# A softmax region reordered: the short last piece of q and k first, the square root by log and exp, no diagonal matrices

## The chip, the cores and the metric

The kernel runs on one core of a Trainium2 chip. The metric is the device time of one execution in microseconds; the kernel before was run three times. Engines: PE multiplies matrices (its weight loads are listed as PEld), DVE is VectorE, ACT ScalarE, SP the engine that issues most DMAs.

## What is computed

```python
qn = q / (norm(q, axis=tokens) + 1e-6)        # q, k, v: 6080 x 256
kn = k / (norm(k, axis=tokens) + 1e-6)
s = kn.T @ qn / tau                           # 256 x 256
a = softmax(s)                                # rows, sum + 1e-9
x = v @ a                                     # 6080 x 256
x = square(relu(x @ w_in_1)) @ w_out_1        # 256 -> 2048 -> 256
h = x @ w_in_2
out = (h * clip(h + 3, 0, 6) / 6) @ w_out_2
```

## The kernel before

The weights arrive as 64-bit floats. Each half of a 512-column block of them is loaded by SP (L269) into one of two buffers (tag `w64`) and made single precision by a *conversion* of three background steps: Abs and a scaled copy on ACT (L135, L136), clamp and shift on DVE (L123, L127), add and sign on DVE (L139, L131). The sign step still reads the raw words, so a buffer is free for the next load when it has run. Halves of `w_out` have two steps more: the rounded part `hi` on ACT (L105) and the remainder `lo` on DVE (L295).

**Score region.** q and k come in pieces of 2, then 4, then 3 and 2 tiles of 128 rows, and a last short one of 64 rows. For each tile PE adds k^T q into two PSUM tiles (L510; one such 32-bit matmul is two records in the trace), ACT squares (L535, L538), DVE adds the squares up (L111). After a piece `STEPS` says how many background steps run. The matmuls of the last 4 tiles are held back (`HELD`).

**Softmax region.** Square sums by PE (L560), guard (L566), square root on ACT (L568), one Newton step and reciprocals on DVE, two diagonal matrices (L579), from which PE makes the row `factor` (L584); the held scores fill PE. Then per half `dh`: scale (L599), maximum (L601), Exp with its sum (L602), two transposes (L610), a copy to `e_sb` (L611). `attn_w(u)` multiplies the softmax matrix with block `w1[u]` of the first weights (L442, four products); `take` (L449) scales the result into the block `wblk`, and `hi[a]`, `lo[a]` split it into the slots of `w_ops[0, u]`. `parts` and the rest's steps prepare the data's slots in the same way from `blk`. Background steps stand between all this at five places (`FILL`).

**Steps.** After that the kernel runs (phase, chunk, u, p) steps. A step of the first kind has 24 products with `w_ops` (`mul`, L712), squares of Relu (L744 to L748), `hi` and `lo` of the result, and 24 products of the step before with `w_out` (L654), in the order that `out_mms` gives: the first ones use the second half of `w_out`'s block. In step 0 there is no step before; the four products of `attn_w(1)` are put in its place, spread by `AW_POPS`. Step 1 starts with `need(("o", 0))`, the conversions of `w_out`'s block 0.

**Order.** PE, SP and GpSimd run in the order of the program throughout. In the softmax region ACT and DVE do too, up to `ordered.close()`; behind it the planner places their work by readiness and then by order, and may put it into gaps ahead. `background(n)` takes the next n steps of two alternating tasks; `beside` inside a step calls it for a share of what is due; `need(name)` runs a task to its end. A task's load is issued when it becomes one of the first two.

## Time and profile before

| | us |
|---|---|
| median of three runs | 1073.31 (1073.2 to 1073.48) |
| span of the profiled execution, first to last instruction | 1071.5 |
| PE busy | 1064.3 (99%) |
| DVE busy | 889.3 (83%) |
| ACT busy | 640.7 (60%) |

The span is that of one profiled execution; a run's time has some 1.8 us around it. PE's busy time counts pipelined matmuls, so it doesn't show short waits; they are read from the distance of its records and from the waits of its weight loads.

### The profile page before, as it was taken

The page shows a single profiled execution, that of the slowest core. Times are in us where ns is not written, and L with a number is a line of the kernel's source. Part 1 is how long each engine was busy: PE and PEld are TensorE (multiplying, and loading weights), DVE is VectorE, ACT ScalarE, POOL GpSimd, SP SyncE. Part 2 cuts the span into 40 slices and gives each one's busy share as a digit, 9 for nine tenths or more (in the row PEclk, how much of TensorE's full clock was granted, in tenths as well). Part 3 has the DMA queues.
Part 4 walks back from the last instruction along what each step waited for, and adds up shares of the span by engine and source line. Part 5 has one row for each costly group of instructions (what it writes and reads, how often), then busy time and mean ns, then how long its engine had stood idle before and what let it go on. Part 6 is the DMA issues. An engine that isn't in the chain of part 4 may idle for free.

```text
span 1071.5 us, 12778 instructions
## 1 busy us (share of the span) xinstructions
PE 1064.3 (99%) x4602; PEld 866.0 (81%) x4602; DVE 889.3 (83%) x1510; ACT 640.7 (60%) x1111; POOL 9.4 (1%) x22
## 2 busy tenths in 40 slices
PE   9999999999999999999999999999999999999998
PEld 8777788888888888888888888888888888888886
DVE  5999958877887987887868988898898898898785
ACT  6699756666666567666555455455555555555443
POOL 0000000000000000000100000000000000000000
PEclk9999999999999999999999999999999999999999
DMA  9624302113132113115435002002002001001001
GB/s 356 247 93 143 98 20 69 60 62 115 50 115 81 50 59 132 45 59 197 138 137 186 1 0 78 1 1 78 1 1 79 1 1 61 18 0 39 1 1 39
DMA packets 33567, 78.03 MB, mean 73 GB/s; under 512 B 3296, under 2 KB 16864, under 8 KB 33504
## 3 DMA queue, kind: packets, MB, share of 16 engines
q1 hardware_dynamic: 27024, 57.49, 16.2%
q0 software_dynamic: 2304, 11.54, 3.2%
q10 hardware_dynamic: 4176, 8.19, 2.1%
q8 instruction: 36, 0.59, 0.2%
q14 instruction: 27, 0.22, 0.1%
HBM read 53.22 MB, written 23.99 MB: 72 GB/s over the span
## 4 chain that ended last, share of the span: by engine, by line
PE 95%; DMA 3%; DVE 1%; ACT 1%; issue 0%; SPq 0%; ACTq 0%; DVEq 0%
PE y L654 50%; PE s L712 44%; DMA q<-q_dram 2%; PE s L442 1%; DMA k<-k_dram 1%; ACT sq L538 0%; PE aw L442 0%; DVE acck L111 0%; DVE accq L111 0%; ACT cv L136 0%; DVE mx L601 0%; DVE sc L599 0%; DVE w L131 0%; DVE ct L139 0%; DVE b L108 0%
## 5 line engine op out<-in xcount | busy, mean ns | idle before, releaser
L654 PE MATMUL y<-g,oh 128*128 128x506 f32 (+1 forms) x1536 | 507.5, 392 | 0.0
L712 PE MATMUL s<-b,wh 128*128 128x506 f32 (+1 forms) x1360 | 424.8, 394 | 0.0
L108 DVE TENSOR_TENSOR g<-h,g 128x506 fp32r<-128x506 f32 (+1 forms) x384 | 262.4, 684 | 106.7 <-ACT g L105 98.7
L654 PEld LDWEIGHTS y<-g,oh 128*128 128x128 f32 x1536 | 289.5, 189 | 64.0 <-DVE g L108 0.4
L712 PEld LDWEIGHTS s<-b,wh 128*128 128x128 f32 x1360 | 255.9, 188 | 61.0 <-issue 1.9
L654 PE MATMUL y<-g,ol 128*128 128x506 f32 (+1 forms) x768 | 302.3, 394 | 0.0
L712 PE MATMUL s<-b,wl 128*128 128x506 f32 (+1 forms) x680 | 267.5, 393 | 0.0
L105 ACT ACTIVATE g<-h 128x506 fp32r<-128x506 f32 (+1 forms) x384 | 235.3, 622 | 38.1 <-DVE h L757 14.1
L105 ACT ACTIVATE u<-s 128x506 f32<-128x506 f32 (+1 forms) x176 | 104.6, 594 | 134.7 <-PE s L712 134.7
L654 PEld LDWEIGHTS y<-g,ol 128*128 128x128 f32 x768 | 144.7, 188 | 31.5
L712 PEld LDWEIGHTS s<-b,wl 128*128 128x128 f32 x680 | 128.4, 189 | 28.2 <-DVE wl L108 0.2
L111 DVE TENSOR_TENSOR h<-u,s 128x506 f32<-128x506 f32 (+1 forms) x176 | 119.5, 679 | 23.7 <-ACT u L105 22.3
L105 ACT ACTIVATE m<-s 128x506 f32<-128x506 f32 (+1 forms) x88 | 52.3, 595 | 114.4 <-PE s L712 113.9
L740 DVE SCALAR_TENSOR_TENSOR h<-r,h 128x506 f32<-128x506 f32 (+1 forms) x144 | 98.9, 687 | 4.9
L736 DVE SCALAR_TENSOR_TENSOR h<-h 128x506 f32<-128x506 f32 (+1 forms) x120 | 81.9, 683 | 1.4
L756 ACT ACTIVATE r<-s,three 128x506 f32<-128x506 f32 (+1 forms) x48 | 32.9, 685 | 60.3 <-PE s L712 59.9
L111 DVE TENSOR_TENSOR h<-m,s 128x506 f32<-128x506 f32 (+1 forms) x88 | 59.9, 680 | 8.0 <-PE s L712 3.2
L739 DVE TENSOR_SCALAR r<-h 128x506 f32<-128x506 f32 (+1 forms) x144 | 60.6, 421 | 1.7
L108 DVE TENSOR_TENSOR b<-blk,b 128x506 fp32r<-128x506 f32 (+1 forms) x81 | 55.0, 681 | 0.0
L105 ACT ACTIVATE b<-blk 128x506 fp32r<-128x506 f32 (+1 forms) x81 | 49.5, 615 | 0.4 <-DMA blk<-vT_dram 0.4
L753 ACT ACTIVATE r<-s 128x506 f32<-128x506 f32 (+1 forms) x40 | 23.8, 594 | 38.1 <-PE s L712 34.0
L510 PE MATMUL sc<-q,k 128*128 128x256 f32 x192 | 43.3, 384 | 0.7 <-DMA q<-q_dram 0.5
(85 smaller groups left out, 495.4 us busy)
## 6 DMA issues: line engine op xcount, KB each, us to landing
w<-w_in_dram SPq DMA_DIRECT2D x16, 512.0 KB, 4.7
w<-w_out_dram SPq DMA_DIRECT2D x16, 512.0 KB, 3.8
k<-k_dram SPq DMA_DIRECT2D x10, 512.0 KB, 7.4
blk<-vT_dram SPq DMA_DIRECT2D x8, 506.0 KB, 6.6
y<-y ACTq DMA_DIRECT2D x16, 253.0 KB, 2.8
blk<-y SPq DMA_DIRECT2D x8, 506.0 KB, 5.0
outT_dram<-y SPq DMA_DIRECT2D x15, 253.0 KB, 2.1
q<-q_dram SPq DMA_DIRECT2D x7, 512.0 KB, 8.1
```

What stands on the lines that cost most here:

```text
L105: ACT.activation(out=out, in_=in_, func=AF.Copy)
L108: DVE.tensor_tensor(out=out, in0=a, in1=b, op=ALU.subtract)
L111: DVE.tensor_tensor(out=out, in0=a, in1=b, op=ALU.add)
L442: return lambda: PE.matmul(ps[dh], e_sb[dh][:, eh], w1[u][:, eh], start=(eh == 0), stop=(eh == 1))
L510: return lambda: PE.matmul(s_ps[dh][:, :C], t["k"][:n, b, dh * P:(dh + 1) * P], t["q"][:n, b], start=first, stop=last)
L654: PE.matmul(y_ps[ph, c, b, e][:, :n], w[:, j, e * P:(e + 1) * P], x, start=start, stop=stop)
L712: PE.matmul(dst, w[:, a, rows], x, start=first and k == 0, stop=k == 2, skip_group_check=True)
L736: DVE.scalar_tensor_tensor(out=h, in0=h, scalar=0.0, in1=h, op0=ALU.max, op1=ALU.mult)
L739: DVE.tensor_scalar(out=r, in0=h, scalar1=3.0, scalar2=0.0, op0=ALU.add, op1=ALU.max)
L740: DVE.scalar_tensor_tensor(out=h, in0=r, scalar=6.0, in1=h, op0=ALU.min, op1=ALU.mult)
L753: ACT.activation(out=r, in_=x, func=AF.Relu)
L756: ACT.activation(out=r, in_=x, func=AF.Relu, bias=three)
```

## The change

The 64-row piece is loaded and used first, into tiles of its own; q's queue is ACT for it. The last piece comes q first. One score of the first half and five of the second are held back. The square sums, guards and norms of q and k are made one after the other; the square root of n is Exp(0.5 Ln(n)), from one table loaded at the start; the factor's row is a matmul with the reciprocals broadcast as weights. The second copy to `e_sb` goes to ACT. The rest's data steps are written into the region's order instead of being a background task. `FILL` has two places instead of five and `STEPS` one step less. The slots of `w_ops[0,0]` are split in another order; the first product of step 0's second result is moved ahead; the products of `attn_w(1)` follow step 0. Background steps traced behind the region are issued after the last `hi` and `lo` of `w_ops[0,0]` on their engine (`gate`), until step 8. The diff, cut to its core:

```diff
-LOADS = ("", "", "0", "t", "1", "", "", "m", "", "", "", "", "", "v")
-STEPS = (0, 0, 0, 1, 1, 1, 1, 1, 1, 1, 0, 0, 0, 0)
-HELD = 4
-FACTOR_AT = 4
-CHAIN = "bo"
+LOADS = ("", "", "", "0", "t", "1", "", "", "m", "", "", "", "", "v")
+STEPS = (0, 0, 0, 0, 1, 1, 1, 1, 1, 1, 0, 0, 0, 0)
+HELD = (1, 5)
+CHAIN = "o"
 SLOTS = 12
-FILL = (1, 1, 2, 2, 3)
-WARM = (8, 0, 2)
+FILL = (1, 1)
+WARM = (4, 3, 2)
...
-AW_POPS = (1, 2, 2, 1)
...
+                for ins in gate:
+                    behind.enter_context(tc.issue_after(ins))
...
-        if u == 1:
-            ps = [psy.tile([P, 512], F32, tag=f"y0{dh}", name="aw") for dh in range(2)]
-        else:
-            ps = [bank([P, 512]) for _ in range(2)]
+        ps = [bank([P, 512]) for _ in range(2)]
...
-    pieces = [(False, sum(sizes[:i]), g) for i, g in enumerate(sizes)]
-    if REM:
-        pieces.append((True, 0, 1))
+    pieces = [(True, 0, 1)] * (REM > 0) + [(False, sum(sizes[:i]), g) for i, g in enumerate(sizes)]
+    LEAD = REM > 0
...
+        rest_tiles = {t: atp.tile([P, 1, C], F32, name="rest" + t) for t in "qk"}
...
+            for nm in "qk" if i == len(pieces) - 1 else "kq":
                 queue = ACT if i < 4 and nm == "q" else SP
                 if rest:
-                    SP.dma_start(out=t[nm][:REM, 0], in_=srcs[nm][J * P:, :])
+                    t[nm] = rest_tiles[nm]
+                    queue.dma_start(out=t[nm][:REM, 0], in_=srcs[nm][J * P:, :])
                 else:
+                    t[nm] = qkp.tile([P, G, C], F32, tag=nm, name=nm)
...
-        ACT.activation(out=tiny, in_=ones[:, :1], func=AF.Sqrt)
+        ACT.preload_act_table_set("natural_log_exp_and_others")
...
+                for dh in range(2):
+                    f = score(dh, t, n, b, tile_at == 0, tile_at == total - 1)
+                    if tile_at < total - HELD[dh]:
+                        f()
+                    else:
+                        scores[dh].append(f)
                 tile_at += 1
-                if tile_at <= total - HELD:
-                    run(f)
-                else:
-                    scores.append(f)
+            if rest:
+                warm(WARM[1])
+                for nm in "kq":
+                    DVE.memset(acc[nm][REM:, 0], 0.0)
...
-            if i == len(pieces) - 3:
+            if i == len(pieces) - 2:
...
-            else:
-                add_data("rest", 0, 0, ("b12", 0), 1)
...
+        def guard(nm):
+            x = cols[nm]
+            DVE.tensor_scalar(out=n2[:, x], in0=n_ps[:, x], scalar1=2.0 ** -100, scalar2=0.25, op0=ALU.max,
+                              op1=ALU.mult)
+        def norm(nm):
+            x = cols[nm]
+            ACT.activation(out=nrm[:, x], in_=n2[:, x], func=AF.Ln)
+            ACT.activation(out=nrm[:, x], in_=nrm[:, x], func=AF.Exp, scale=0.5)
+            DVE.reciprocal(out=rec[:, x], in_=nrm[:, x])
+            DVE.tensor_tensor(out=rec[:, x], in0=rec[:, x], in1=n2[:, x], op=ALU.mult)
+            DVE.scalar_tensor_tensor(out=nrm[:, x], in0=rec[:, x], scalar=1e-6, in1=nrm[:, x],
+                                     op0=ALU.add, op1=ALU.add)
...
+        last_rows("q")
+        one_row("q")
+        square_sums("q")
+        last_rows("k")
+        guard("q")
+        one_row("k")
+        run(scores[0])
+        run(scores[1][:1])
+        square_sums("k")
+        run(scores[1][1:2])
         background(FILL[0])
-        n2 = atp.tile([P, 4], F32, name="n2")
-        DVE.tensor_scalar(out=n2, in0=n_ps[:, :4], scalar1=2.0 ** -100, scalar2=None, op0=ALU.max)
-        nrm = atp.tile([P, 4], F32, name="nrm")
-        ACT.activation(out=nrm, in_=n2, func=AF.Sqrt)
-        ACT.activation(out=tiny, in_=ones[:, :1], func=AF.Exp)
-        rec = atp.tile([P, 4], F32, name="rec")
-        DVE.reciprocal(out=rec, in_=nrm)
-        DVE.tensor_tensor(out=rec, in0=rec, in1=n2, op=ALU.mult)
-        add(nrm, nrm, rec)
-        DVE.tensor_scalar(out=nrm, in0=nrm, scalar1=0.5, scalar2=1e-6, op0=ALU.mult, op1=ALU.add)
+        norm("q")
         DVE.reciprocal(out=rec[:, 2:], in_=nrm[:, 2:])
-        diag = atp.tile([P, 2, P], F32, name="diag")
+        f_ps = bank([P, 512])
         for h in range(2):
-            DVE.tensor_scalar(out=diag[:, h], in0=ident, scalar1=rec[:, 2 + h:3 + h], scalar2=None, op0=ALU.mult)
+            PE.matmul(f_ps[:, h * P:(h + 1) * P], rec[:, 2 + h:3 + h].to_broadcast([P, P]), ident, start=True, stop=True)
+        run(scores[1][2:])
+        guard("k")
+        norm("k")
         DVE.tensor_scalar(out=nrm[:, :2], in0=nrm[:, :2], scalar1=tau_sb, scalar2=None, op0=ALU.mult)
         DVE.reciprocal(out=rec[:, :2], in_=nrm[:, :2])
-        warm(WARM[1])
-        f_ps = bank([P, 512])
-        PE.matmul(f_ps[:, :C], ones, diag.rearrange("p h e -> p (h e)"), start=True, stop=True)
-        run(scores[FACTOR_AT:])
-        warm(WARM[2])
         parts = data_prep(data[0, 0], chunks[0][1], (1, 2), new_slot(0, 0))
-        parts[0]()
         factor = atp.tile([P, C], F32, name="factor")
         copy_act(factor, f_ps[:, :C])
-        parts[2]()
-        background(FILL[1])
+        parts[0]()
+        warm(WARM[2])
...
-                parts[1]()
+                parts[2]()
...
-            DVE.tensor_scalar(out=e_sb[dh], in0=t_ps[dh], scalar1=1.0, scalar2=None, op0=ALU.mult)
+            if dh == 0:
+                DVE.tensor_scalar(out=e_sb[dh], in0=t_ps[dh], scalar1=1.0, scalar2=None, op0=ALU.mult)
+            else:
+                copy_act(e_sb[dh], t_ps[dh])
+        rest_parts = data_prep(data[0, 0], chunks[0][1], ("b12", 0), new_slot(0, 0))
+        finished.add(("rest", 0, 0))
+        rest_parts[0]()
+        rest_parts[2]()
         transposed(0)
+        parts[1]()
+        parts[3]()
         run(products[:1])
-        parts[3]()
-        background(FILL[2])
         transposed(1)
         run(products[1:])
         DVE.tensor_scalar(out=rsum, in0=sm, scalar1=1e-9, scalar2=None, op0=ALU.add)
         DVE.reciprocal(out=rsum, in_=rsum)
-        background(FILL[3])
+        background(FILL[1])
...
+            ahead = []
...
-                x = bank()[:, :n]
-                mul(x, ms[0], True)
+                if ahead:
+                    x = ahead.pop()
+                else:
+                    x = bank()[:, :n]
+                    mul(x, ms[0], True)
                 if i == 0 and k == 0:
-                    pop(1)
+                    ahead.append(bank()[:, :n])
+                    mul(ahead[0], (3, 1), True)
...
-                pop(AW_POPS[k] if i == 0 else PLAIN_POPS[k])
+                pop(PLAIN_POPS[k])
...
-    hi[1]()
-    lo[1]()
-    take[1]()
-    hi[2]()
-    lo[2]()
-    background(FILL[4])
-    for f in (hi[3], lo[3], hi[0], lo[0]):
+    for f in (hi[1], lo[1], hi[3], lo[3], rest_parts[1], take[1], hi[2], lo[2]):
         f()
+    chain_end = hi[0](), lo[0]()
+    rest_parts[3]()
     finished.add(("w", 0, 0))
     ordered.close()
+    gate.extend(x.ins for x in chain_end)
...
-        if not prev:
-            need(("w1", 1))
-            products, take = attn_w(1)
-            outs = [(f, None) for f in products]
-        else:
+        if prev:
             if prev[0][0] == 0 and prev[0][1] == 0:
                 need(("o", prev[0][2]))
             outs = out_mms(*prev[0], prev[1])
         if i == MANUAL_FROM:
+            gate.clear()
...
-            if u:
-                products, before = attn_w(u + 1)
-                run(products)
-            else:
-                before = take
+            products, before = attn_w(u + 1)
+            run(products)
```

## Rows read from the trace of the kernel before

**Rows 1.** The page: the chain that ended last, by engine.

```profile
PE 95%; DMA 3%; DVE 1%; ACT 1%; issue 0%; SPq 0%; ACTq 0%; DVEq 0%
```

**Rows 2.** Windows: start:end, length, busy us (count) by engine, clock, DMA share, GB/s.

```profile
20.00:30.00 10.00, 9.86 (x46) 8.40 (x45) 9.93 (x12) 8.68 (x10) 0.00 (x0) 1.00 1.03 409
...
44.00:56.00 12.00, 11.29 (x45) 6.46 (x44) 10.93 (x33) 8.28 (x18) 0.00 (x0) 1.00 0.25 82
...
110.00:120.00 10.00, 10.00 (x39) 6.86 (x38) 10.00 (x20) 8.16 (x15) 0.00 (x0) 1.00 0.40 109
```

**Rows 3.** Waits of PEld from 62 us on: total us, times, longest us.

```profile
PEld s L442 <- issue: 2.6, 11, 0.2
...
PEld y L654 <- DVE g L108: 0.4, 1, 0.4
```

**Rows 4.** Timeline of the start, PE: start us, us, operation, [idle before <- releaser].

```profile
1.06 3.78 PE L473 MATMUL s<-ones 128*128 128x128 f32 x16 [1.06 <-DVE three L428]
...
4.63 2.19 PE L510 MATMUL sc<-q,k 128*128 128x256 f32 x8
...
7.33 2.86 PE L510 MATMUL sc<-q,k 128*128 128x256 f32 x12 [0.52 <-DMA q<-q_dram]
```

**Rows 5.** Timeline of PE, 42 to 67 us.

```profile
44.24 0.61 PE L560 MATMUL s<-ones,acck 128*128 128x1 f32 x4
...
47.38 0.70 PE L584 MATMUL s<-diag,ones 128*128 128x256 f32 x2
...
49.93 0.71 PE L473 MATMUL s<-ones 128*128 128x128 f32 x4
...
51.66 1.12 PE L442 MATMUL s<-w,e 128*128 128x512 f32 x2 [0.64 <-DVE e L611]
...
55.78 0.73 PE L712 MATMUL s<-b,wh 128*128 128x508 f32 x2
...
66.23 0.39 PE L654 MATMUL y<-g,oh 128*128 128x508 f32 x1
66.46 0.40 PE L654 MATMUL y<-g,ol 128*128 128x508 f32 x1
```

**Rows 6.** Timeline of DVE, 42 to 67 us.

```profile
45.33 0.16 DVE L566 TENSOR_SCALAR n<-s 128x4 f32<-128x4 f32 x1
...
46.85 0.48 DVE L579 TENSOR_SCALAR diag<-ident,rec 128x128 f32<-128x128 f32 x2
...
48.29 0.69 DVE L131 SCALAR_TENSOR_TENSOR w<-w,ct 128x512 uint32<-128x512 uint32 x1
48.90 0.48 DVE L599 SCALAR_TENSOR_TENSOR sc<-sc,rec,factor 128x256 f32<-128x256 f32 x1
...
54.85 0.69 DVE L131 SCALAR_TENSOR_TENSOR w<-w,ct 128x512 uint32<-128x512 uint32 x1
...
57.32 1.28 DVE L108 TENSOR_TENSOR b<-blk,b 128x508 fp32r<-128x508 f32 x2
...
65.53 0.68 DVE L295 TENSOR_TENSOR ol<-cv,oh 128x512 fp32r<-128x512 f32 x1
```

**Rows 7.** Timeline of ACT, 42 to 67 us.

```profile
45.75 1.28 ACT L569 ACT_TABLE_LOAD   x1
...
48.12 0.38 ACT L105 ACTIVATE factor<-s 128x256 f32<-128x256 f32 x1 [0.36 <-PE s L584]
...
53.49 0.64 ACT L135 ACTIVATE ct<-w 128x512 f32<-128x512 f32 x1
...
59.46 0.68 ACT L135 ACTIVATE ct<-w 128x512 f32<-128x512 f32 x1 [0.53 <-DMA w<-w_out_dram]
60.05 0.66 ACT L136 ACTIVATE cv<-w 128x512 int32<-128x512 uint32 x1
...
64.77 0.64 ACT L105 ACTIVATE oh<-cv 128x512 fp32r<-128x512 f32 x1
```

**Rows 8.** Timeline of SP around 55.6 us.

```profile
55.60 0.37 SPq L269 DMA_DIRECT2D w<-w_out_dram  x1
```

More of the change, by code (lines that the diff above doesn't have):

```diff
@@ L540, in tile_channel_attention_then_two_ffn @@
             filled += m
+            if final:
+                assert m == 0 and g == G // 2 == width and not rest
+                continue
             for b in range(0, g - m, width):
@@ L559, in tile_channel_attention_then_two_ffn @@
             for h in range(2):
-                PE.matmul(n_ps[:, 2 * i + h:2 * i + h + 1], acc[nm][:, 0, h * P:(h + 1) * P], ones[:, 0:1],
-                          start=True, stop=True)
-        scores = [f[dh] for dh in range(2) for f in scores]
-        run(scores[:FACTOR_AT])
-        background(FILL[0])
-        n2 = atp.tile([P, 4], F32, name="n2")
-        DVE.tensor_scalar(out=n2, in0=n_ps[:, :4], scalar1=2.0 ** -100, scalar2=None, op0=ALU.max)
-        nrm = atp.tile([P, 4], F32, name="nrm")
```

38 lines of the change are left out of this document (22 added, 16 removed).

## The prediction

> **What bounds the kernel now.** I read the chain of work that ended last first, then the engines' busy time by windows, then the waits, then TensorE, VectorE, ScalarE and SyncE in order of time around the softmax. The chain lies 95% on PE [rows 1]. After 62 us only PE's weight loads wait at all, never more than 0.4 us at a time [rows 3]; so from there the end moves with the time at which PE may start, unless a new wait appears. Before that, PE waits twice: 0.52 us for the second piece at 7.33 [rows 4], and between the square sums (44.24) and the first product with `w_ops[0,0]` (55.78) [rows 5]. In those 11.54 us PE has some 8.6 us of work: 16 score records at 0.216, eight square-sum records (0.9), two of the factor (0.43), transposes (0.4) and eight records of the first weight product at 0.43. The rest, 2.9 us, is all that a better softmax can give back there.
>
> The second thing to see is VectorE: 10.93 of 12 us busy in the softmax, 10.00 of 10 still at 110 to 120 [rows 2]. It is full of background steps, the conversions of the weights, and the planner also pulls later ones forward: the Abs at 53.49 belongs to the first half of `w_out` (task `("o", 0)`, taken in step 0) and sits inside the softmax [rows 7]. The third is what these steps feed. A raw weight occupies one of two buffers until its sign step (L131) has run. The sign step of w1[1]'s second half ends at 54.85 + 0.69 = 55.54 [rows 6]; SyncE issues the load of `w_out`'s second half at 55.60 [rows 8], ScalarE waits for it until 59.46 [rows 7], and its low part is written at 65.53 + 0.68 = 66.21 [rows 6]. The L654 that reads it starts at 66.46 [rows 5]. Margin 0.25 us: this chain is as late as it may be.
>
> **The change part by part.**
>
> *Start.* The short piece now comes first: 131 KB more ahead of the large pieces, 0.32 us at 409 GB/s [rows 2], and one more issue on each queue. PE meets it in its first waits, but the second large piece lands later by that, so the wait of [rows 4] ends later. From there to the square sums it runs 168 score records in both versions (before 192 - 8 - 16, now 192 - 4 - 8 - 12). **Square sums: 44.24 + 0.35 = 44.6.** VectorE's two 64-row additions leave the end of its chain; cover for what moves to the front is the time in which it has no piece yet, and if that fails it is two more operations of 0.4 us.
>
> *Norm of q.* Four sum records instead of eight before the first guard: 45.33 [rows 6] + 0.35 - 0.45, about 45.25. From guard to the factor's matmul it takes 47.38 - 45.33 = 2.05 now [rows 5, 6]; the two diagonals (row at 46.85, 0.48) go, and a second small activation (about 0.2, as the guard's 0.16 and its hand-over) comes, and the hand-over of the diagonals goes with them: about 1.5 to 1.7, so 46.75 at the earliest. PE has by then run four scores records, k's sums and two more (44.6 + 0.45 + 0.86 + 0.45 + 0.43 = 46.8). No wait, or 0.2 at most. k's guard, two activations and five small operations behind it end at 48.4; `sc` starts there instead of at 48.90 [rows 6], where today the conversion at 48.29 holds it up. The table load costs ScalarE 1.28 us at 45.75 [rows 7], and the next activation that depends on anything waits 0.36 for PE after it: hidden, so its removal is costed at nothing.
>
> By the Trainium skill (ScalarE: Activation LUTs, What ACT_TABLE_LOAD costs), a switch of tables costs about 2.66 us with its drain; were that on the path the result would be 2.7 us lower. The row, 1.28 us and a later wait on PE, says otherwise.
>
> *To the first product.* From `sc` to the first L442 is 51.66 - 48.90 = 2.76 now [rows 5, 6]; one 0.68 us subtraction of data leaves VectorE's queue there: 51.05. Behind it the four products run on without the wait for `e1` (that copy moves to ScalarE, behind two data copies, and is done at 52.85 by the same spacings): 51.05 + 0.53 + 0.43 + 0.22 + 6 x 0.43 = 54.81. `take[0]`, which stood behind the pulled-forward conversion at 53.49, is ready by then. **First L712: 54.8 instead of 55.78, a gain of 0.97.** From there to the first L654 PE has the same records as now (24 + 6 single and 8 double ones, 10.45 us [rows 5]); only the order differs, since w1[1]'s product goes behind step 0. With no new wait PE would reach L654 at 65.3.
>
> *What this is paid with.* Of the 16 background steps done before step 0 now, four are the rest's own, twelve weights'; after it `STEPS` and `FILL` leave eight, the rest's four stand in the written order. w1[1] is left with the add and sign of its first half and all of its second half; the gate forbids them, and those of `("o", 0)`, to start before the last `lo` of `w_ops[0,0]`. That is queued behind `take[1]` (54.97 + 0.7), `hi[2]`, `hi[0]`: VectorE issues it at 56.5 and is free at 56.82. Queued on VectorE then, by spacings of 0.60 for a 512-column pair operation ([rows 6], two in 1.28) and 0.335 for a one-input one: the rest's `lo` 0.60, first half's add and sign 1.20, second half's clamp and shift 0.67, step 0's square, two `lo` and second square 2.40 (they are traced ahead of the last conversion), second half's add and sign 1.20, tail 0.09: **sign step done at 62.98** instead of 55.54. If the conversions went before all of step 0's work it would be 60.58; if three more of step 0's operations came ahead, 64.78. PE needs w1[1] at 60.5 (54.8 and 24 records of 0.23), so it waits there first, and everything behind in its order with it; that wait lies within the next one.
>
> Behind the sign step hangs the load of `w_out`'s second half. Sign end to Abs took 59.46 - 55.54 = 3.92; Abs and scaled copy 60.05 + 0.66 - 59.46 = 1.25 [rows 7]; add 0.69, sign 0.69, `hi` 0.64, `lo` 0.68 and four hand-overs of 0.04 (the one to SyncE above takes 0.06) are 2.86 [rows 6, 7]. Together 8.03; with other work between, as now, 66.21 - 55.54 = 10.67. I take the lower, because PE will stand and so nothing competes on ScalarE and VectorE. **62.98 + 8.03 = 71.01, so L654 with it at 71.05 instead of 66.46: 4.6 us later.** The ends are 60.58 + 8.03 (2.2 later) and 64.78 + 10.67 (9.0 later); both delays together are unlikely when PE waits, so I cut the upper to 7. What follows (w1[2], `w_out` 1) shifts by about as much as PE does.
>
> **The sum.** The profile's span is 1071.5; the median of the runs is 1073.31, 1.8 more, which lie outside the span and don't change. 1073.31 + 4.6 = 1077.9; own range 1075.5 to 1080.5.
>
> **The rivals.**
>
> *Not slower: the conversions fit after all.* If w1[1]'s last sign step is done by 57.4 (65.3 - 8.0), L654 finds its weight, and PE's own arithmetic stands: 0.97 gained, 1072.3. For it: VectorE gets some 4 us of gaps in the new softmax. Against: the gate keeps these steps out of just those gaps, and from 56.82 there is no room for 3.1 us of them by 57.4. With PE's softmax waits gone altogether (2.9 less the 0.35 at the start) it would be 1070.8.
>
> *The clock falls in the new waits.* PE stands from 60.5 to 63 and again before 71, about 2.5 us each; today's longest is below 1 us and the granted clock stays at 1.00 of its upper level, 2.4 GHz [rows 2]. At the start the warming matmuls have 16 records in 3.78 us, later four in 0.71 [rows 4, 5]: 0.22 apart against 0.11, once the overlap of the last is taken off, so PE ran at 1.2 GHz for about 4 us from its beginning. Another such stretch costs half of that: 1077.9 + 2.1 = 1080.0. The Trainium skill (TensorE: Matmul & The Clock Gate, What's actually happening) says that an idle array falls back to the throttled clock; no row here shows it at waits of this size.
>
> *The activation tables change more often.* If Ln and Exp got different tables, three loads of 1.28 [rows 7] would enter the norm chain, q's and k's: some 3 us later up to step 0 and all behind it, 1081. The Trainium skill (ScalarE: Activation LUTs, Table sets) lists one set that has both, which speaks against it.
>
> **How the numbers follow.** Forecast 0.62; not slower 0.25 (0.17 at 1072.3, 0.08 near 1070.8); clock 0.08; tables 0.05. About 0.2% (2.1 us) is what a measurement can tell from no change. Slower 0.74 (forecast, clock and tables, less 0.01), same 0.16, faster 0.10. The range runs from the not slower case, 1072.2, to 1080.5.
>
> **What would show it.** In the changed kernel's trace: square sums near 44.6 and the first L712 near 54.8 (steps 1 to 3); no table load after the start; PE waiting some 2.5 us for the sign step L131 ahead of the L442 of w1[1], around 60 to 63; the second `w_out` load issued near 63; and the first L654 waiting for the operand `oh`/`ol`, near 71. If L654 starts at 66 or before, the prediction is wrong in the step on what the gain is paid with.

## The result, and the profile after

The changed kernel takes 1083.52 us in the median of four runs (1081.3 to 1083.95), beside 1073.37 for the kernel before: a ratio of 1.0092 with a 95% interval of 1.008 to 1.0104. The profiled execution is the one of 1081.3 us; its span is 1079.5, so the 1.8 us outside the span are as before and the span grew by 8.0. The other three have spans of 1081.5 to 1082.2 and a lower mean granted clock (0.994 to 0.996 against 0.998). The forecast was 1077.9, 4.6 more than before, and the range ended at 1080.5. The kernel is slower, as foretold, and through the two waits that were foretold, but by 10.15 us.

In the fences below line numbers are those of the kernel after: L507 the scores (L510 before), L575 the square sums (L560), L439 the weight products (L442), L743 the products of the first layer (L712), L685 the outputs (L654), L129 the sign step (L131), L296 the low part of `w_out` (L295). In the experiments with added lines they are up to seven higher.

PE at the start, in order of time (start us, us, operation, [idle before <- releaser]); it answers [rows 4]:

```profile
1.06 2.08 PE L469 MATMUL s<-ones 128*128 128x128 f32 x8 [1.06 <-DVE ones L427]
3.42 2.07 PE L507 MATMUL sc<-restq,restk 64*128 64x256 f32 x4 [0.28 <-DMA restq<-q_dram]
5.42 1.65 PE L469 MATMUL s<-ones 128*128 128x128 f32 x6
6.86 4.35 PE L507 MATMUL sc<-q,k 128*128 128x256 f32 x17
```

Four score records take 2.07 us here; at full clock four take 1.13 (experiment 4). PE therefore still runs at 1.2 GHz in its first score records, and the trace's clock records have the rise at 7.90 us, where the kernel before has it at 5.21.

PE from the square sums on; it answers [rows 5]:

```profile
45.36 0.50 PE L575 MATMUL s<-ones,accq 128*128 128x1 f32 x4
...
50.66 0.44 PE L635 MATMUL s<-ident,sc 128*128 128x128 f32 x2 [0.76 <-ACT sc L627]
51.61 1.13 PE L439 MATMUL s<-w,e 128*128 128x512 f32 x2 [0.52 <-DVE e L637]
...
55.05 0.95 PE L743 MATMUL s<-b,wh 128*128 128x508 f32 x2
...
64.41 2.84 PE L439 MATMUL s<-w,e 128*128 128x512 f32 x6 [2.36 <-DVE w L129]
...
72.63 0.70 PE L685 MATMUL y<-g,oh 128*128 128x508 f32 x1 [4.00 <-ACT oh L103]
73.63 0.79 PE L685 MATMUL y<-g,ol 128*128 128x508 f32 x1 [0.30 <-DVE ol L296]
...
84.12 0.39 PE L685 MATMUL y<-g,oh 128*128 128x508 f32 x1
```

The softmax did what it should: from the square sums to the first product 9.69 us instead of 11.54 [rows 5], so the first product comes 0.73 earlier although the sums are 1.12 later. Then PE stands twice, 2.36 us for the weight w1[1] and 4.00 and 0.30 for the second half of `w_out`, which before it met without a stop [rows 3, 5]. The last line is the 24th output, the end of the first group. The kernel before has it here:

```profile
75.71 0.39 PE L654 MATMUL y<-g,oh 128*128 128x508 f32 x1
```

That is 8.41 us later, and the span is 8.0 longer: the whole difference is made before 84 us. From the first product to the 24th output PE takes 29.07 us instead of 19.93, 9.14 more. Of these, 7.13 lie ahead of the first output (17.58 instead of 10.45) and 2.01 behind it (11.49 instead of 9.48). The clock has its part in the second, as the third of these windows shows (length, busy us and count of PE, PEld, DVE, ACT, POOL, then clock, DMA share, GB/s; compare [rows 2]):

```profile
44.00:56.00 12.00, 10.73 (x51) 7.68 (x50) 8.29 (x28) 7.36 (x20) 0.00 (x0) 1.00 0.04 14
...
62.00:70.00 8.00, 4.27 (x13) 2.19 (x12) 6.96 (x13) 6.19 (x12) 0.00 (x0) 1.00 0.44 148
...
72.00:76.00 4.00, 3.08 (x7) 2.12 (x8) 3.86 (x7) 2.25 (x6) 0.00 (x0) 0.59 0.44 131
```

As PE starts again at 72.63 its granted clock falls from 2.4 to 1.2 GHz, and the clock records hold it there for 3.41 us (72.75 to 76.16): half of that, 1.7, is lost, and with the stop of 0.30 it makes the 2.01. The 7.13 are the stops of 2.36 and 4.00 and 0.8 more. Some 0.3 of this is overlap that a stop takes away: an output record of 0.39 us is followed by the next after 0.23 [rows 5], so that a stop costs more than the idle time that the profile lists. The rest is slower records, mostly the first product. The first window shows where the payment comes from: VectorE is busy 8.29 of 12 us beside the softmax, 10.93 before, and the 2.6 us of work that are missing are done later, while PE waits for them.

VectorE where the debt is paid; it answers [rows 6]:

```profile
57.43 0.68 DVE L106 TENSOR_TENSOR b<-blk,b 128x508 fp32r<-128x508 f32 x1
58.02 0.68 DVE L137 CUSTOM_DVE_ANT_0 ct<-ct,cv 128x1024 uint16<-128x1024 uint16 x1
...
63.07 0.68 DVE L779 TENSOR_TENSOR h<-r 128x508 f32<-128x508 f32 x1
63.67 0.68 DVE L129 SCALAR_TENSOR_TENSOR w<-w,ct 128x512 uint32<-128x512 uint32 x1
...
69.13 0.42 DVE L121 TENSOR_SCALAR ct<-ct 128x512 f32<-128x512 f32 x1
69.59 0.43 DVE L125 TENSOR_SCALAR ct<-ct 128x512 uint32<-128x512 uint32 x1
70.15 0.69 DVE L137 CUSTOM_DVE_ANT_0 ct<-ct,cv 128x1024 uint16<-128x1024 uint16 x1
70.88 0.69 DVE L129 SCALAR_TENSOR_TENSOR cv<-w,ct 128x512 uint32<-128x512 uint32 x1
72.08 0.43 DVE L121 TENSOR_SCALAR ct<-ct 128x512 f32<-128x512 f32 x1 [0.51 <-ACT ct L133]
72.55 0.43 DVE L125 TENSOR_SCALAR ct<-ct 128x512 uint32<-128x512 uint32 x1
72.89 0.68 DVE L296 TENSOR_TENSOR ol<-cv,oh 128x512 fp32r<-128x512 f32 x1
```

and ScalarE on the same chain; it answers [rows 7]:

```profile
68.39 0.66 ACT L133 ACTIVATE ct<-w 128x512 f32<-128x512 f32 x1
...
71.39 0.66 ACT L133 ACTIVATE ct<-w 128x512 f32<-128x512 f32 x1
71.96 0.61 ACT L103 ACTIVATE oh<-cv 128x512 fp32r<-128x512 f32 x1
```

The sign step of w1[1]'s second half ends at 63.67 + 0.68 = 64.35. Only then may the raw buffer be loaded again with the second half of `w_out`; its Abs starts at 68.39, its clamp, shift, add and sign at 69.13 to 70.88, its high part at 71.96, its low part ends at 72.89 + 0.68 = 73.57, and PE's output with it starts at 73.63. In front of the low part stand two steps of a weight that is needed only later (72.08 and 72.55).

### The profile page after: what moved, and what is told of

Same layout as the page of the kernel before. It is cut to its first block, busy times and chain, and to the rows that moved or that the text cites. A ratio compares the mean times of both kernels' runs of the same rounds, so it can differ in the third digit from the quotient of the medians.

```text
span 1079.5 us, 12775 instructions
## 1 busy us (share of the span) xinstructions
PE 1065.8 (99%) x4602; PEld 867.1 (80%) x4602; DVE 890.7 (83%) x1510; ACT 643.4 (60%) x1112; POOL 9.4 (1%) x22
## 3 DMA queue, kind: packets, MB, share of 16 engines
q0 software_dynamic: 2304, 11.54, 3.2%
## 4 chain that ended last, share of the span: by engine, by line
PE 97%; DVE 1%; ACT 1%; DMA 1%; issue 0%; ACTq 0%; DVEq 0%
PE y L685 49%; PE s L743 43%; PE sc L507 4%; PE s L439 1%; DMA w<-w_in_dram 0%; DMA restq<-q_dram 0%; PE s L469 0%; ACT ct L133 0%; DVE g L106 0%; ACT wblk L446 0%; ACT r L775 0%; ACT wh L103 0%; DVE ol L296 0%; DVE ct L137 0%; PE s L635 0%
## 5 line engine op out<-in xcount | busy, mean ns | idle before, releaser
L685 PE MATMUL y<-g,oh 128*128 128x506 f32 (+1 forms) x1536 | 508.3, 393 | 4.0 <-ACT oh L103 4.0
L743 PE MATMUL s<-b,wh 128*128 128x506 f32 (+1 forms) x1360 | 424.1, 393 | 0.0
L685 PEld LDWEIGHTS y<-g,oh 128*128 128x128 f32 x1536 | 289.9, 189 | 68.8 <-ACT oh L103 4.4
L743 PEld LDWEIGHTS s<-b,wh 128*128 128x128 f32 x1360 | 255.9, 188 | 60.1 <-issue 1.4
L685 PE MATMUL y<-g,ol 128*128 128x506 f32 (+1 forms) x768 | 302.7, 394 | 0.3 <-DVE ol L296 0.3
L743 PE MATMUL s<-b,wl 128*128 128x506 f32 (+1 forms) x680 | 267.3, 393 | 0.0
L685 PEld LDWEIGHTS y<-g,ol 128*128 128x128 f32 x768 | 144.8, 189 | 32.4 <-DVE ol L296 0.8
L743 PEld LDWEIGHTS s<-b,wl 128*128 128x128 f32 x680 | 128.3, 189 | 28.3 <-DVE wl L106 0.2
L787 ACT ACTIVATE r<-s,three 128x506 f32<-128x506 f32 (+1 forms) x48 | 32.9, 686 | 60.5 <-PE s L743 60.1
L770 DVE TENSOR_SCALAR r<-h 128x506 f32<-128x506 f32 (+1 forms) x144 | 60.5, 420 | 1.7
L507 PE MATMUL sc<-q,k 128*128 128x256 f32 x188 | 41.9, 383 | 0.0
```

The lines of the kernel that those rows point to most:

```text
L507: return lambda: PE.matmul(s_ps[dh][:, :C], t["k"][:n, b, dh * P:(dh + 1) * P], t["q"][:n, b], start=first, stop=last)
L685: PE.matmul(y_ps[ph, c, b, e][:, :n], w[:, j, e * P:(e + 1) * P], x, start=start, stop=stop)
L743: PE.matmul(dst, w[:, a, rows], x, start=first and k == 0, stop=k == 2, skip_group_check=True)
L770: DVE.tensor_scalar(out=r, in0=h, scalar1=3.0, scalar2=0.0, op0=ALU.add, op1=ALU.max)
L787: ACT.activation(out=r, in_=x, func=AF.Relu, bias=three)
```

## The experiments

Theory: the loss is the two waits of PE for weights whose conversion steps no longer run beside the softmax, one behind the other through the raw buffers, and the clock's answer to those waits. Rivals: the start (four warmings instead of eight, the short piece first) carries a good part; the new norm steps themselves cost something; VectorE's list is full, so that work moved back beside the softmax only lengthens it. The 12 kernels, with the kernel before at 1073.3 to 1073.4 beside each:

| kernel | median us (range) | ratio to before (95%) |
|---|---|---|
| after | 1083.52 (1081.3 to 1083.95) | 1.0092 (1.008 to 1.0104) |
| 1 no gate | 1078.1 (1077.03 to 1080.22) | 1.0047 (1.0032 to 1.0061) |
| 2 steps beside the softmax | 1079.58 (1078.92 to 1080.0) | 1.0056 (1.004 to 1.0073) |
| 3 halves of `w_out` swapped | 1081.15 (1080.63 to 1081.93) | 1.0073 (1.0058 to 1.0088) |
| 4 eight warmings | 1081.97 (1081.78 to 1085.9) | 1.0089 (1.0072 to 1.0106) |
| 5 = 2 + 3 + 4 | 1076.64 (1074.6 to 1078.02) | 1.0029 (1.002 to 1.0039) |
| 6 = 4 and PE kept busy in the wait | 1081.82 (1080.91 to 1082.01) | 1.0074 (1.0057 to 1.0091) |
| 7 before, four warmings | 1074.54 (1073.47 to 1075.29) | 1.001 (1.0001 to 1.002) |
| 8 = 5 and outputs in the order of the halves | 1073.61 (1072.59 to 1076.88) | 1.0 (0.9984 to 1.0016) |
| 9 = 8, short piece second | 1073.8 (1073.6 to 1075.89) | 1.0006 (0.9997 to 1.0015) |
| 10 = 4, short piece second | 1084.1 (1083.75 to 1085.23) | 1.0103 (1.0089 to 1.0117) |
| 11 = 8, short piece fifth | 1072.89 (1072.53 to 1073.57) | 0.9996 (0.9987 to 1.0005) |
| 12 before, steps taken out of the softmax | 1075.96 (1075.59 to 1077.19) | 1.0025 (1.0015 to 1.0036) |

**Experiment 1: no gate.** One line of after is removed, so that the background steps need no longer wait for the last low part of `w_ops[0,0]`.

```diff
-    gate.extend(x.ins for x in chain_end)
```

> The changed kernel without the gate: background steps traced behind the softmax region may again be put into gaps ahead of it. Theory 'load chain' (the sign step of w1[1]'s second half frees the raw buffer for the second half of w_out, and the first product with w_out waits for that): the planner pulls the conversions into VectorE's gaps at 44.9 to 45.9 and 53.8 to 55, the sign step moves from 64.4 to about 59 to 61, the product from 73.6 to about 69, time 1077 to 1080. Rival 'VectorE is full' (what the conversions take there, the softmax chain loses): first L743 later than 55.05 by as much as the conversions gain, time 1082 to 1084, no difference.

Measured: 1078.1, 5.4 us less than after. PE, in order of time:

```profile
50.60 0.68 PE L607 MATMUL s<-ident,rec 128*128 128x128 f32 x4 [1.35 <-DVE n L579]
...
58.25 0.86 PE L743 MATMUL s<-b,wh 128*128 128x508 f32 x2
...
70.94 0.49 PE L685 MATMUL y<-g,oh 128*128 128x508 f32 x1 [1.71 <-ACT oh L103]
```

The wait for w1[1] is gone and that for `w_out` is 1.71 instead of 4.00. But the conversion steps now push into the norm chain: an add at 48.76 and a sign step at 49.49 stand between VectorE's operations for q's norm, and PE waits 1.35 for the reciprocals at its end (the profile names the guard of k, which comes just behind them). The first product is at 58.25, 11.35 behind the sums (46.90) instead of 9.69. From there to the 24th output PE takes 24.32 us instead of 29.07. Both sides are true: the gate does cost, and VectorE's list has no free place just anywhere. The profiled execution is the slowest of the four (1080.22).

**Experiment 2: steps beside the softmax, at chosen places.** The gate stays; one more step beside the score pieces, two ahead of q's guard, one moved behind the softmax and one more ahead of step 0.

```diff
-STEPS = (0, 0, 0, 0, 1, 1, 1, 1, 1, 1, 0, 0, 0, 0)
+STEPS = (0, 0, 0, 0, 1, 1, 1, 1, 1, 1, 1, 0, 0, 0)
-FILL = (1, 1)
+FILL = (0, 2)
         last_rows("k")
+        background(1)
+        tasks[1].steps.pop(0)()
         guard("q")
...
     rest_parts[3]()
+    background(1)
```

> The changed kernel with the five conversion steps of w1[1] that it left for later written into the softmax region, where VectorE and ScalarE stood: Abs of the first half as a seventh step of the score region, clamp and shift of it and Abs of the second half before q's guard, two steps after the row sums, the last one behind the rest's low part. Theory 'load chain': second sign step at about 59.3 instead of 64.4, no wait of the L439 of w1[1] (2.4 us now), second w_out load at 59.4 and the product with it at 68 to 68.6 instead of 73.6; no fall of the clock; time 1075 to 1076.5. Rival 'VectorE is full': the first L743 moves from 55.05 to 57 or later and the time stays at 1080 or above.

Measured: 1079.58, 3.9 less than after.

```profile
56.47 0.94 PE L745 MATMUL s<-b,wh 128*128 128x508 f32 x2
...
70.79 0.49 PE L687 MATMUL y<-g,oh 128*128 128x508 f32 x1 [3.36 <-ACT oh L103]
```

The sums are at 46.79, so the softmax takes 9.68 us, as short as in after, with these steps in it; the wait for w1[1] is gone. There is room on VectorE, if the steps stand where the norm chain leaves it. What remains is the second wait, 3.36, and the clock fell behind it, so the 1075 to 1076.5 that I had expected were missed. From the first product to the 24th output PE takes 25.95 us, 3.1 less than in after.

**Experiment 3: halves of `w_out` swapped.** The first group's first outputs need rows 256 to 511 of the weight; after converts rows 0 to 255 first.

```diff
-        for a in (0, 2):
-            add_task(("o", u) if a else None, ...)
+        for i, a in enumerate((2, 0) if u == 0 else (0, 2)):
+            add_task(("o", u) if i else None, ...)
```

> The changed kernel with the halves of w_out's block 0 loaded and converted in the other order, so that the half that the first products use takes the buffer freed by w1[1]'s first sign step (59.95) rather than its second (64.35). Nothing else is moved: the wait for w1[1] (2.4 us) stays. Theory 'load chain': first product with w_out at about 69 instead of 72.6 to 73.6, the next wait for the other half near 72, in all 2.5 to 4 us less and no fall of the clock, 1077.5 to 1080. Rival 'VectorE is full': the two halves are done at the same times as before the swap, the second one decides, and less than 1 us is gained.

Measured: 1081.15, 2.4 less than after.

```profile
69.81 0.50 PE L685 MATMUL y<-g,oh 128*128 128x508 f32 x1
...
74.14 0.50 PE L685 MATMUL y<-g,oh 128*128 128x508 f32 x1 [2.18 <-ACT oh L103]
```

The first output no longer waits for its weight, the seventh does, 2.18. The chain to the second half is as long as before; PE only has more to do until it meets its end. From the first product to the 24th output it takes 27.57 us, 1.5 less than in after; what the medians differ by beyond that is not explained by this trace.

**Experiment 4: eight warmings together.**

```diff
-WARM = (4, 3, 2)
+WARM = (8, 0, 2)
```

> The changed kernel with eight warming matmuls ahead of the short piece and none behind it, instead of four and three, so that PE does not stand between them and the short piece. Measures the part of the loss that the start has: the granted clock rises at 7.9 us in the changed kernel and at 5.2 in the one before, and the square sums start at 45.36 instead of 44.24. Theory 'clock at the start': rise back at about 5.2, square sums at 44.6 to 44.9, and as the load chain behind depends on the same region it comes 0.5 to 0.8 us earlier: 1082.7 to 1083. Rival 'later landing' (131 KB more ahead of the large pieces): square sums stay at 45.2 or later, no difference.

Measured: 1081.97, 1.5 less than after. PE at the start:

```profile
4.77 1.13 PE L507 MATMUL sc<-restq,restk 64*128 64x256 f32 x4
6.35 1.99 PE L507 MATMUL sc<-q,k 128*128 128x256 f32 x8 [0.45 <-DMA q<-q_dram]
8.90 3.29 PE L507 MATMUL sc<-q,k 128*128 128x256 f32 x14 [0.56 <-DMA q<-q_dram]
```

At full clock from the first score record on, PE is ahead of the data and waits 0.45 and 0.56 for them: the sums come at 45.27, hardly earlier than the 45.36 in the profile of after. That is the trace that the rival 'later landing' foretold. Where the clock rises later than in these two, it matters: in the profiles of experiments 1 to 3, with the start of after, the clock records have the rise at 10.1 to 11.0 us and the sums come at 46.6 to 46.9. But it is not shown that the 1.5 us between the medians are the start's. The one run of after with a mean granted clock of 0.998 took 1081.3 us, the two of experiment 4 with 0.998 took 1081.78 and 1081.89; the medians differ because after's other three runs have 0.994 to 0.996. That mean leaves out the half clock ahead of the first rise: the 7.90 us of after's profile would lower it by 0.004, and it is 0.998 with the later fall of 3.41 us alone. So the lower values tell of half clock behind the start (experiment 10).

**Experiment 5: edits 2, 3 and 4 in one kernel.**

> The three edits together: w1[1]'s conversions written into the softmax region, the halves of w_out's block 0 in the other order, eight warming matmuls first. From the runs of the parts: square sums near 45.3 (as with eight warming matmuls) instead of 46.8, so first L743 near 55.0; second sign step near 59.5; the half of w_out that is needed first takes the buffer freed near 54.3 and is ready by 64, the other takes the one freed at 59.5 and is ready near 68.5, needed near 68. Theory 'load chain and clock': PE waits under 1 us behind 55, no fall of the clock, time 1073 to 1075, no worse than the kernel before by more than 0.15%. Rival 'VectorE is full': the waits come back elsewhere in the first three steps and the time is 1077 or more.

Measured: 1076.64, 6.9 less than after, where 3.9 + 2.4 + 1.5 = 7.8; 1073 to 1075 had been expected. From the first product to the 24th output PE takes 23.94 us, 5.1 less than in after, where 2 and 3 by themselves have 3.1 and 1.5 less and 4 has 0.3 more: the parts add up, and a little more. The first output is at 66.13, as early as before. One stop is left:

```profile
69.56 0.50 PE L687 MATMUL y<-g,oh 128*128 128x508 f32 x1 [1.89 <-ACT oh L103]
```

and behind it the clock falls once more for 3.41 us (69.96 to 73.38). 1.89 and half of 3.41 are 3.6; the median is 3.4 above that of before beside it (1073.26).

**Experiment 6: PE kept busy.** Edit 4, and 16 matmuls on ones ahead of the first outputs, in the wait.

```diff
+                if i == 1 and k == 0:
+                    d = bank([P, 512])
+                    for _ in range(16):
+                        PE.matmul(d[:, :P], ones, ones, start=True, stop=True)
```

> The changed kernel with eight warming matmuls first and 16 matmuls of ones more in step 1, where PE waits for w_out (about 68.4 to 72.8): 3.4 us of PE work inside a wait of 4.5, results unused. Measures by itself what the fall of the clock (3.41 us at half, from about 73) costs. Theory 'clock': the record of the granted clock shows no fall, first product with w_out still at 72.8, time 1080 to 1081 instead of 1082. Rival 'the wait alone': the fall costs nothing, as PE has little to do in it; time 1082 as without.

Measured: 1081.82, which can't be told from experiment 4. The window that has 0.59 in after (0.63 in experiment 4):

```profile
72.00:76.00 4.00, 2.86 (x17) 2.18 (x16) 3.24 (x6) 2.63 (x5) 0.00 (x0) 1.00 0.42 132
```

The clock doesn't fall when PE has something to do in the wait, and from the first product to the 24th output PE takes 28.15 us instead of 29.41. In this profile, however, the clock rose only at 9.83 and the sums came at 46.35, 1.08 later than in experiment 4 with the same code up to there. So the saving of 1.26 is seen within one trace; the time is what the rival foretold, 1082, and doesn't show it. That the clock held in all four runs is likely by their mean granted clock, 0.999 in each, against 0.993 to 0.998 in experiment 4.

**Experiment 7: the kernel before with four warmings.** `WARM = (8, 0, 2)` becomes `(4, 0, 2)`, nothing else.

> The kernel before with four warming matmuls instead of eight, nothing else: PE then stands from about 2.8 us to the landing of the first pieces near 4.5. Measures by itself what the start of the changed kernel (clock up at 7.9 to 10.9) costs. Theory 'clock at the start': clock up at 8 to 11 us instead of 5.2, square sums at 46 to 47 instead of 44.24, time 1074.5 to 1075.8. Rival 'landing': the pieces land as before, PE catches up in its later waits for them, square sums within 0.5 us of 44.24, time 1073.4.

Measured: 1074.54, 1.3 more than before beside it (1073.26). The start and the sums:

```profile
4.53 7.69 PE L510 MATMUL sc<-q,k 128*128 128x256 f32 x21 [1.40 <-DMA q<-q_dram]
...
45.51 0.56 PE L560 MATMUL s<-ones,acck 128*128 128x1 f32 x4
```

PE stands 1.40 us behind the warmings, the clock rises at 10.41, the sums come 1.27 later [rows 5], at 45.51 where I had expected 46 to 47; the time follows one for one. This edit costs the kernel before 1.3 us by itself (interval of the ratio 1.0001 to 1.002).

**Experiment 8: outputs in the order of the halves.** Experiment 5, and the first group's 24 outputs ordered so that the twelve which need only the converted half go first; the first stretch takes six of them, not seven.

```diff
-        for k, (i, b) in enumerate(((1, 1), (0, 1), (0, 0), (1, 0))):
+        at_0 = (ph, c, u) == (0, 0, 0)
+        for k, (i, b) in enumerate(((1, 1), (1, 0), (0, 1), (0, 0)) if at_0 else ...):
...
-                pop(PLAIN_POPS[k])
+                pop((6 if i == 1 else PLAIN_POPS[k]) if k < 3 else PLAIN_POPS[k])
```

> The version with three edits to the kernel after (two more conversion steps beside the softmax, the halves of the first w_out converted in the order the first group of outputs can take, eight warmings together) and a fourth: the first group's outputs that need only the converted half go first (twelve of its 24, six of them in the first stretch), those of the other half last. Waits theory (what is left of the loss are the stops of TensorE for the second half of w_out, 1.89 us at 69.56 in that version's profile, and 1.7 us for the half clock in the 3.41 us behind it): no idle of TensorE over 0.6 between 56 and 80, no fall of the clock, first part of the other half's outputs at about 71.5 without a wait; 1076.6 - 3.5 = 1073.1 (1072.3 to 1074.3), about the kernel before. Rival, VectorE's list is the bound whatever the order: the same wait is found at a later product or output in 70 to 80, and the time stays at 1075.5 to 1077.

Measured: 1073.61, 9.9 less than after and no longer to be told from before. The windows:

```profile
62.00:70.00 8.00, 8.00 (x30) 5.24 (x29) 7.13 (x14) 7.95 (x16) 0.00 (x0) 1.00 0.42 129
70.00:80.00 10.00, 10.00 (x45) 8.16 (x44) 9.87 (x19) 8.41 (x16) 0.00 (x0) 1.00 0.38 107
```

PE is busy without a gap where after has 4.27 of 8, and the clock stays at 1.00. From the first product to the 24th output it takes 20.25 us, against 29.07 in after and 19.93 before. Square roots by logarithm and exponential, no diagonals and the short piece first are all still in this kernel: none of them costs what after lost. From the sums to the first product this execution takes 10.30 us, 0.62 more than those of experiments 5, 9 and 11 with the same steps (9.68 to 9.69). VectorE's last step for the second half:

```profile
69.95 0.69 DVE L296 TENSOR_TENSOR ol<-cv,oh 128x512 fp32r<-128x512 f32 x1 [0.70 <-ACT oh L103]
```

This low part ends at 70.64, 2.93 earlier than in after, and is asked for only behind the twelve outputs of the other half.

**Experiments 9 and 10: the short piece second.** Experiments 8 and 4, each with the short piece of q and k behind the first full piece (`pieces.insert(1, (True, 0, 1))`).

> As the run above, with the short piece of q and k loaded and used second instead of first. Start theory (with the short piece first TensorE waits for it and again for the first full pieces: scores at 6.75, a stop of 0.55 at 9.30, square sums at 45.66, where the kernel before has 4.63 and 44.24): scores from about 4.6, square sums at 44.3 to 44.8, so 1.0 less than the run above: 1072.1 (1071.3 to 1073.1), faster than the kernel before by 0.1%. Rival, the 16 DMA engines limit the start whatever the order (their share is 1.0 in 10 to 30): sums stay at 45.3 to 45.7 and the time within 0.3 of the run above.

> The kernel after with eight warmings together and the short piece second, to be held against the run with eight warmings and the short piece first (1081.97, sums at 45.27). Start theory: sums at 44.3 to 44.8, 1081.2 (1080.5 to 1081.6), with the wait of 2.36 for w1[1], that of about 4.3 at the first output and the fall of the clock unchanged. Rival (DMA limits the start): sums at 45.2 to 45.4 and 1082.0. Waits theory, for the end of the stretch: as TensorE comes 0.8 earlier to the same waits on VectorE, whose work doesn't start earlier, some of the 0.8 is given back: 1081.5 to 1082.

Measured: 1073.8 and 1084.1. The start of experiment 9:

```profile
4.90 2.37 PE L509 MATMUL sc<-q,k 128*128 128x256 f32 x8
7.20 1.13 PE L509 MATMUL sc<-restq,restk 64*128 64x256 f32 x4
9.35 2.86 PE L509 MATMUL sc<-q,k 128*128 128x256 f32 x12 [1.02 <-DMA q<-q_dram]
```

The scores begin earlier, but PE then stands 1.02 for the next full piece, and the sums come at 46.37, 0.78 later than in experiment 8. My start theory was wrong in this form: the second place brings nothing over the first. Experiment 10 is 2.1 above experiment 4, where I had expected a gain or none. Its profile shows more than the start (sums at 46.01): the clock falls at both waits, 3.41 us from 64.77 and 6.83 us from 75.01.

```profile
76.00:80.00 4.00, 4.00 (x10) 3.13 (x10) 3.58 (x8) 1.25 (x2) 0.00 (x0) 0.50 0.21 83
```

The mean granted clock of this execution is 0.995, its span 1083.5. The longer runs of after have 0.994 to 0.996. A mean of 0.996 over their 1082 us is a loss of 3.8 to 4.9 us; the fall in after's profile makes up 1.7 of it, and the fall at the very end of a run, which takes at most 3.2 us ahead of the last instruction in these traces, 1.6. So these runs lost at least 0.5 us more to the clock behind the start than the profiled one, which fits a further fall. Where it lay no trace shows, and a late rise may have come on top.

**Experiment 11: the short piece fifth.** Experiment 8, with the short piece behind four full ones, the loads and steps beside the pieces (`LOADS`, `STEPS`) moved accordingly.

> The version with the four edits (1073.61; square sums at 45.59, with stops of TensorE of 0.8 at 9.06 and 0.3 at 6.24, DMA moving 284 GB/s in the first 10 us against 306 in the kernel before), with the short piece of q and k loaded and used fifth, when full pieces are already queued. Start theory in its second form (small transfers early leave the 16 DMA engines less full, and the first full pieces come late for it; neither first nor second place avoids that): scores from 4.6, first 10 us at 300 GB/s or more, square sums at 44.6 to 44.9 (44.24 of the kernel before and the two products more that stand ahead of the sums, 0.43), 1072.7 (1071.9 to 1073.4). Rival (the start is bound by the sum of bytes, and the rest of the 1.3 us lies elsewhere): sums at 45.3 to 45.7, 1073.3 to 1074. Against both: where the conversions don't start earlier with it, TensorE comes early to them and waits, and the gain at the start is given back by the 24th output (76.1 in the run above).

Measured: 1072.89, the lowest median of all, 0.48 under before, with an interval (0.9987 to 1.0005) that holds 1: no gain is shown.

```profile
4.63 7.73 PE L509 MATMUL sc<-q,k 128*128 128x256 f32 x29
...
45.18 0.50 PE L579 MATMUL s<-ones,accq 128*128 128x1 f32 x4
...
54.87 0.94 PE L750 MATMUL s<-b,wh 128*128 128x508 f32 x2
```

No wait for data is left at the start, perhaps in part because the clock rose only at 6.38 here (5.64 in experiment 8) and PE was slower until then. The first 10 us move 309 GB/s. The other profiles bear this out whenever their clock rose: 281 to 286 GB/s with the short piece first (after, 1 to 6, 8), 277 and 261 with it second (9, 10), 306 and 307 with it last (before, 7, 12). So small transfers among the first do hold up the full pieces. The sums come 0.41 earlier than in experiment 8, half of what I had expected; that the later clock takes the rest is likely, not shown.

**Experiment 12: the kernel before with seven steps out of the softmax.** `FILL = (1, 1, 2, 2, 3)` becomes `(1, 1, 0, 0, 0)`.

> The kernel before (square roots, diagonal matrices, short piece last: all as it was) with one thing of the change: seven background steps (conversions and splits of weights and data) that it takes beside the softmax, after the square sums, are left to the first products. Order theory (the loss comes from when VectorE and ScalarE do the conversions, not from how the norms are computed): first product 0.5 to 1.5 earlier than 55.78, then a wait for w1[1] of 0 to 2.5 and one of 2 to 5 for the first outputs (66.23 before, 70 to 73 here), with or without a fall of the clock, 1077 to 1082. Rival (the loss needs the new norm steps, the gate or the short piece): no wait, 1073 to 1074.

Measured: 1075.96, and not in the way of either theory.

```profile
46.56 0.69 DVE L131 SCALAR_TENSOR_TENSOR w<-w,ct 128x512 uint32<-128x512 uint32 x1
...
48.57 0.70 PE L584 MATMUL s<-diag,ones 128*128 128x256 f32 x2 [0.92 <-DVE diag L579]
49.48 0.69 DVE L131 SCALAR_TENSOR_TENSOR w<-w,ct 128x512 uint32<-128x512 uint32 x1
...
53.09 0.41 PE L610 MATMUL s<-ident,sc 128*128 128x128 f32 x2 [1.26 <-ACT sc L602]
...
58.10 0.73 PE L712 MATMUL s<-b,wh 128*128 128x508 f32 x2
```

The steps were put off in the program's text and came earlier in the trace: the sign steps stand at 46.56 and 49.48 instead of 48.29 and 54.85 [rows 6], between the operations of the norm chain and right ahead of `sc`. The kernel before has no gate, and as in experiment 1 I read this as the planner's doing, which takes a step that is not written into the order as soon as its operands are there; that reading was not tested further. PE waits for the diagonals and the exponential, the first product is 2.32 later [rows 5], behind it nothing waits, and the time is 2.6 longer. So the experiment did not test the order theory; it gives the price of the same conversions in the wrong place, and suggests what the gate of the change is good for.

## Why the prediction was right, and where it was not

Two steps of the sum failed. For the way from the sign step to the low part it took the shortest value, 8.03 us, "because PE will stand and so nothing competes"; 9.22 were measured. And it put the fall of PE's clock at nothing, as a rival beside the forecast; the fall came with the waits and cost 1.7. The sign step was mis-sized besides, by 1.37. The upper bound was cut to 7 because "both delays together are unlikely"; they came together and made 7.17.

*Start (44.6 foretold, 45.36 measured).* Mis-sized. I counted 131 KB more at the full rate, 0.32 us, and nothing for the four warmings that are taken away at the front. In the profile of after PE stands between warmings and scores and runs the first scores at half clock; at full clock it waits for data instead (experiment 4), so 0.7 us are lost either way. With a still later rise the sums come at 46.6 to 46.9, and experiment 7 shows 1.3 us for fewer warmings alone. The wait for the first data hides the time of the warmings themselves, but not the later rise of the clock when PE stands in their place. Of the 0.76 only 0.25 is left at the first product.

*Norm chain and softmax.* Right: `sc` at 49.03 (48.4 foretold, with the start 0.76 late), first product at 55.05 (54.8 foretold), no table load in the chain. The step from `sc` to the first weight product, 2.65 in the forecast, doesn't follow from the two numbers given for it (2.76 less 0.68 is 2.08); 2.58 were measured. That the removed table load gives nothing was not tried by itself; the 1.85 us that the softmax became shorter are the sum of the diagonals, the load, the order and the conversions that left it. PE still waits there, 0.76 for the exponential and 0.52 for VectorE's copy.

*Payment, the sign step (62.98 foretold, 64.35 measured).* Right in kind, PE's first wait 2.36 where I had 2.5; late by 1.37. That the wait agrees is in part luck: PE came late to it too, and stands from 62.05 instead of 60.5 (54.8 and 24 records of 0.23 are 60.3), as two of the eight records of the weight product ran ahead of it. VectorE reaches the rest's low part at 57.43 instead of 56.82 (0.61); one more square of step 0 (63.07) goes ahead of the sign step than I had counted (0.60); a clamp takes 0.45 in the list where I had 0.335, and small pieces make up the rest. My upper bound, three operations more, was the better value.

*From the sign step to the low part (8.03 foretold, 9.22 measured).* The load and its landing agree (4.04 against 3.92). From the Abs to the end of the low part it took 73.57 - 68.39 = 5.18 instead of 4.11. Some 0.5 of the difference is no competition at all: the weight's own clamp and shift (69.13, 69.59) stand between its Abs and its add (70.15, 1.76 behind the Abs), and the sum left them out and counted Abs, scaled copy and one hand-over, 1.29. The other 0.6 is what the assumption denied. The planner gives the idle engines other weights' steps: an Abs at 71.39 ahead of the high part, which starts 0.39 behind the sign step, and a clamp and a shift at 72.08 and 72.55 ahead of the low part, which starts 0.32 behind the high part, where the sum has 0.04 for each. An engine that others wait for is not idle. The first output with the low part is at 73.63 instead of 71.05: 7.2 later than before, where the forecast had 4.6 and its cut upper bound 7.

*The clock.* I had it as a rival (0.08, 2.1 us) that takes the place of the forecast. It is a consequence of the forecast: behind waits of 1.71 to 4.31 us the clock fell at the outputs in all seven of the profiles that have the wait there and nothing done in it (after, 1 to 5, 10). It belonged into the sum with nearly all the chance of the forecast. The Trainium skill (TensorE: Matmul & The Clock Gate, What's actually happening) says that an idle array falls back to the throttled clock; I had cited it and then followed the row, though no row had a wait of this size, which is just where a row can't speak against a page. The traces agree with it now, with one limit: the wait of 2.36 for w1[1] left the clock at 1.00 in after and in experiments 3, 4 and 6, and lowered it in 10.

*The sum.* By the profile the forecast's 4.6, 1.4 for the sign step and 1.2 for the way to the low part make 7.2 at the first output with it; 1.2 of the clock's loss fall behind that output and make 8.4 at the 24th; 8.0 are left at the end. The median is 2.2 further up than the profiled execution. The lower mean granted clock of the longer runs speaks for a further fall there (experiment 10); where it lay remains open.

*The rivals.* "The conversions fit after all" failed in after but not in principle: experiment 8 brings them to fit and gives 1073.6, experiment 11 1072.9. I had 1072.3 for it, from a start of 44.6 that none of these kernels has. Tables: excluded, no load after the start.

## What to carry to other kernels

Work that runs beside a latency-bound stretch is paid for there; if the stretch is shortened by moving that work out, ask for each piece who waits for it, through which buffer, and what the planner will put in front of it later. Here the time and order in which weights are converted, and the order in which products ask for them, were worth 8.8 us between the first product and the 24th output (29.07 in after, 20.25 in experiment 8; the clock's 1.7 are in it), and the softmax became shorter by 1.85 (after; 1.24 in the one execution of experiment 8). When a forecast contains waits of several us on TensorE, put the fall of its clock into the sum, not beside it.

## What the runs showed of the hardware

The granted clock of TensorE fell behind waits of 1.71, 1.89, 2.18, 3.36, 3.83, 4.00 and 4.31 us among the first seven outputs, each time within 1.5 us of the restart, and stayed at 1.2 GHz for 3.41 us six times and 6.83 us once. It did not fall in four of five cases behind the single wait of 2.3 to 2.4 at w1[1] (after, 3, 4 and 6; it fell in 10), and not where 16 matmuls on ones stood in the wait (experiment 6).

After 16 warming records on end the clock rose at 4.7 to 6.8 us in eight of nine profiles (before, 4, 5, 8 to 12) and at 9.83 in one (6); after eight records with a stop behind them at 7.9 to 11.0 in all five (after, 1, 2, 3, 7). The same code gave 4.74 and 9.83, so a single profile doesn't settle what a start costs.
